# A fused attention and MoE kernel: sread of the first batch moved into the second, its state transposes and token sums re-placed, and its start reordered

## The chip, the cores and the metric

One core of one Trainium2 chip runs the whole program. The metric is device microseconds of that core for one execution, as the median of several. The profile is of one such execution; its span is 1.8 us shorter than the time of its run (222.8 against 224.57 for the kernel before).

All times inside an execution are microseconds from the start of its span. Engine names are the profile's: PE is TensorE, DVE is VectorE, ACT is ScalarE, POOL is GpSimd, SP is the engine that issues the transfers of the outputs and the x transposes by DMA. To evict a result is to copy it from the PSUM bank that a matmul wrote to SBUF; a transfer lands when its completion is recorded.

## The reference, cut to what matters

```python
B, H, S, Ns, D = 8, 8, 512, 32, 64
a     = softmax(scale * x @ state.T)          # over Ns, tokens read the state
xread = a @ state                             # [B, H, S, D]
a2    = softmax(scale * state @ x.T)          # over S, the state reads tokens
sread = a2 @ x                                # [B, H, Ns, D]
h     = rows_of(concat([xread, sread])) @ w_in     # 4352 rows, 512 -> 2048
out   = (h * sigmoid(h)) @ w_out                   # 2048 -> 512
```

For the rows of xread the kernel never forms `xread`: it folds the state into the first weight, W1 = state @ w_in for each batch, and feeds `a` (transposed) to it. So each batch b of 0 to 7 needs scores, exp and a normalisation, W1 in four pieces of 512 columns, 16 steps "ft" of G1 (two matmuls of 512 columns, then SiLU on ACT) and 64 matmuls of G2. The rows of sread are kept as `xmT` and form a ninth, smaller batch at the end.

## The kernel before

The parts that the change and the argument touch. `bank` hands out PSUM banks in turn; `both` is (DVE, ACT); `keep_busy(n, ...)` issues n matmuls on a dummy tile, whose result nobody reads. Parts that are left out are marked with `...`.

```python
def token_sums(b):                       # DVE only, about 2.7 us
    for hg in range(2):
        nc.vector.tensor_reduce(f[:, hg], exp_nat[b, hg] ..., op=ADD)
    nc.vector.tensor_copy(es[b][:, 0], f[:])
    nc.vector.tensor_tensor(es[b][:, 1], f[:], es[b][:, 0], op=SUB)

def sread(b):                            # PE 0.68 us, then DVE about 3.0 us
    ps = bank(...)
    ...  # 2 matmuls of 256 columns with es[b], 16 of 64 columns with x_nat[b] and exp_nat[b]
    nc.vector.reciprocal(rb[:], ps[:, 1, :, :, :])
    ...  # four tensor_tensor products into xmT; the bank is held until they are done

def w1_cols(b, cols, engs):              # one piece: 8 matmuls into two banks, evicted by DVE and ACT
    ...

# start of batch 0
keep_busy(7, psH, "h1"); copy(st0); transpose st0; copies into stT (DVE); keep_busy(4, ...)
cast_x(0, nc.vector, h0=0, nh=4);  pe_transpose_x(0, 0, ...)
cast_x(0, nc.vector, h0=4, nh=4)
scores(0, 0); exps(0, 0)
pe_transpose_x(0, 1, ...);  scores(0, 1); exps(0, 1)
...                                       # SiLU table, normalisation, first 256 columns of W1
pe_transpose_a(0, 0, nc.vector); pe_transpose_a(0, 1, nc.vector)

W0 = {0: (256, 256), 2: (512, 512), 6: (1024, 512), 10: (1536, 512)}
for ft in range(NFT):                     # batch 0
    upto(...)                             # G1 steps that are due
    if ft in W0: w1_cols(0, [W0[ft]], both)
    if ft == 1:  token_sums(0)
    if ft == 4:  sread(0)
    if ft == 5:  transpose_state()        # states of batches 1 to 7
    if ft == 6:  evict_state(0, nc.vector)
    if ft == 8:  evict_state(1, nc.vector)
    if ft == 12: cast_x(1, nc.vector); load_x(2)
    if ft in (9, 11, 12): w1_chunks(1, ({9: 0, 11: 1, 12: 2}[ft],), both)
    if ft == 14: ...                      # transposes of x of batch 1 on PE
    if ft < 14:
        for tt in range(3): G2(0, tt, ft)
```

Transfers: x of batch n+1 is loaded in float32 into the single buffer `x_f` by POOL's queue, cast to bf16 (`x_nat`) and transposed (`xT`), on PE for batches 0 and 1, by DMA from SP's queue from batch 2 on.

The softmax here doesn't subtract the row's maximum and nothing guards it: scores larger than these inputs give would overflow.

Of the kernel before, what the change touches and what calls it, by code (L numbers as in the profile page):

```python
# [8 lines left out]
FP32 = mybir.dt.float32  # L9
BF16 = mybir.dt.bfloat16  # L10
AX = mybir.AxisListType.X
# [25 lines left out]
def kernel(  # L37
# [11 lines left out]
    ctx.enter_context(tc.manual_schedule())  # L49

    pers = ctx.enter_context(tc.tile_pool(name="pers", bufs=1))
    xpool = ctx.enter_context(tc.tile_pool(name="xpool", bufs=2))
    xtpool = ctx.enter_context(tc.tile_pool(name="xtpool", bufs=2))
    att = ctx.enter_context(tc.tile_pool(name="att", bufs=4))
    wpool = ctx.enter_context(tc.tile_pool(name="wpool", bufs=2))
# [41 lines left out]
    def cast_x(b, eng, c0=0, nc_=4, h0=0, nh=H):  # L97
        if b not in x_nat:
            x_nat[b] = xpool.tile([128, 4, H, D], BF16, tag="x_nat", name=f"x_nat{b}")
        eng.tensor_copy(  # L100
            x_nat[b][:, ds(c0, nc_), ds(h0, nh), :],
            x_f[:, ds(h0, nh), ds(c0, nc_), :].rearrange("p h c d -> p c h d"),
        )
# [22 lines left out]
    def keep_busy(n, pool, tag):  # L126
        ps = pool.tile([128, 512], FP32, tag=tag, name="ps_busy")
        for _ in range(n):
            nc.tensor.matmul(  # L129
                ps[:], busy[:, 0:128], busy[:], start=True, stop=True, skip_group_check=True  # L130
            )
# [24 lines left out]
    )  # L156


    keep_busy(7, psH, "h1")
    copy(nc.vector, st0_n[:], st0_f[:])  # L160
    ps0 = bank([128, 4, NS], BF16, "ps_st0")
    for kt in range(4):
# [3 lines left out]
    for g in range(2):  # L166
        for u in range(2):
# [2 lines left out]
                stT[ds(64 * u, 64), 0, ds(2 * g, 2), u ^ g, :],  # L170
                ps0[ds(64 * u, 64), ds(2 * g, 2), :],
            )
    keep_busy(4, psH, "h1")




    def pe_transpose_x(b, hg, nb=2, new=bank, engs=(nc.vector, nc.scalar)):
        if b not in xT:
            xT[b] = xtpool.tile([128, 4, 4, 128], BF16, tag="xT", name=f"xT{b}")  # L180
        m = 4 // nb
        for u in range(nb):
            ps = new([128, m, 2, 128], BF16, "ps_xt")
            for i in range(m):
                for j in range(2):
                    nc.tensor.transpose(
                        ps[:, i, j, :],
                        x_nat[b][:, m * u + i, ds(4 * hg + 2 * j, 2), :],
                        ident[:],
                    )  # L190
            copy(engs[u], xT[b][:, ds(m * u, m), ds(2 * hg, 2), :], ps[:])

    cast_x(0, nc.vector, h0=0, nh=4)
    pe_transpose_x(0, 0, 2, lambda sh, dt, nm: psO.tile(sh, dt, tag="o", name=nm))
    cast_x(0, nc.vector, h0=4, nh=4)

    st_ps = []

# [37 lines left out]
                    skip_group_check=True,  # L236
                )

    def exps(b, hg):
        e = att.tile([128, 4, 4, NS], BF16, tag="exp", name="exp_nat")  # L240
        exp_nat[b, hg] = e
        nc.scalar.activation(e[:], sc_ps[hg][:], func=EXP, bias=0.0, scale=SCALE)  # L242

    an = {}

    def norm(b, hg, parts=((nc.gpsimd, 0, 4),)):
        e = exp_nat[b, hg]
        rs = att.tile([128, 4, 4, 1], FP32, tag="rs", name="rs")
        rc = att.tile([128, 4, 4, 1], FP32, tag="rc", name="rc")
        a = att.tile([128, 4, 4, NS], BF16, tag="an", name="an")  # L250
        an[b, hg] = a
        nc.vector.tensor_reduce(rs[:], e[:], axis=AX, op=ADD)  # L252
        nc.vector.reciprocal(rc[:], rs[:])  # L253
        for eng, c, n in parts:
            eng.tensor_tensor(  # L255
                a[:, ds(c, n)],
                e[:, ds(c, n)],
                rc[:, ds(c, n)].to_broadcast([128, n, 4, NS]),
                op=MULT,
            )  # L260
        if hg == 0:
            aT[b] = att.tile([128, 2, 4, 128], BF16, tag="aT", name="aT")
# [91 lines left out]
    gt = {}  # L354
    outs = {}

    def emit_G1(k):
        b, ft = divmod(k, NFT)
        ps = psH.tile([128, 512], FP32, tag="h1", name="h1")
        if b < B:  # L360
            for hg in range(2):
                nc.tensor.matmul(  # L362
                    ps[:],
                    W1[b][:, hg, ds(128 * ft, 128)],
                    aT[b][:, hg, :, :],
                    start=(hg == 0),
                    stop=(hg == 1),
                    skip_group_check=True,
                )
        else:  # L370
            for kt in range(4):
                nc.tensor.matmul(  # L372
                    ps[:, 0:256],
                    w_in_sb[:, kt, ds(128 * ft, 128)],
                    xmT[:, :, kt].rearrange("p t n b -> p t (n b)"),
                    start=(kt == 0),
                    stop=(kt == 3),
                    skip_group_check=True,
                )
        n = 512 if b < B else 256  # L380
        g = gpool.tile([128, 512], BF16, tag="g", name="g")
        gt[k] = g
        nc.scalar.activation(g[:, 0:n], ps[:, 0:n], func=SILU, bias=0.0)  # L383
# [45 lines left out]
    def upto(k):  # L429
        while done[0] < min(k, (B + 1) * NFT):  # L430
            emit_G1(done[0])
            done[0] += 1

    scores(0, 0)
    exps(0, 0)
    pe_transpose_x(0, 1, 2, lambda sh, dt, nm: psH.tile(sh, dt, tag="h1", name=nm))
    scores(0, 1)
    exps(0, 1)
    nc.scalar.activation(warm[:], warm[:], func=SILU, bias=0.0)
    norm(0, 0)  # L440
    norm(0, 1, ((nc.gpsimd, 0, 2), (nc.vector, 2, 2)))
    w1_cols(0, [(0, 256)], (nc.scalar, nc.scalar))
    load_w_in(1024)
    load_w_out(8, 4)
    load_w_in(1536)
# [1 line left out]
    load_x(1)  # L447
    keep_busy(4, psO, "o")
    pe_transpose_a(0, 0, nc.vector)
    pe_transpose_a(0, 1, nc.vector)  # L450



# [5 lines left out]
    for ft in range(NFT):  # L459
        upto(min(ft + LEAD0[ft], ready))  # L460
        if ft in W0:
            w1_cols(0, [W0[ft]], both)
            ready = sum(W0[ft]) // 128
        if ft == 1:
            token_sums(0)
        if ft == 4:
            sread(0)
        if ft == 5:
            transpose_state()
        if ft == 6:  # L470
            evict_state(0, nc.vector)
        if ft == 8:
            evict_state(1, nc.vector)
        if ft == 12:
            cast_x(1, nc.vector)
            load_x(2)
        if ft in (9, 11, 12):
            w1_chunks(1, ({9: 0, 11: 1, 12: 2}[ft],), both)
        if ft == 14:
            nc.scalar.activation(warm[:], warm[:], func=EXP, bias=0.0)  # L480
            pe_transpose_x(1, 0, 1, engs=(nc.vector,))
            pe_transpose_x(1, 1, 1, engs=(nc.scalar,))
        if ft < 14:
            for tt in range(3):
                G2(0, tt, ft)
# [33 lines left out]
    for b in range(1, B):  # L519
        n = b + 1  # L520
        lead = 4 if b == 1 else 6
        for tt in range(4):
            for ft in range(NFT):
                at = (tt, ft)
                if tt == 0:
                    upto(NFT * b + min(lead + ft, NFT))
                    if b == 1 and ft == 2:
                        token_sums(1)
                if b == 1 and at == (1, 4):
                    sread(1)  # L530
                if n < B:
                    if at == (0, NFT - lead):
                        scores(n, 0)
                        scores(n, 1)
                        exps(n, 0)
                        exps(n, 1)
                        nc.scalar.activation(warm[:], warm[:], func=SILU, bias=0.0)  # L537
                    if at == (1, 0):
                        for hg in range(2):
                            norm(n, hg)  # L540
                            transpose_a(n, hg)
                        if n + 1 < B:
                            for c in range(4):
                                cast_x(n + 1, nc.gpsimd, c, 1)
                        if n + 2 < B:
                            load_x(n + 2)
                    if at == (1, 8):
                        token_sums(n)
                    if at == (3, 8):
                        if n + 1 < B:  # L550
                            transpose_x(n + 1)
                    if at == (3, 10):
                        sread(n)
                    if at == (2, 8):
                        w1_chunks(n, (0, 1), both)
                    if at == (3, 4):
                        w1_chunks(n, (2, 3), both)
                    if tt == 3 and ft % 2 == 1 and ft // 2 < 6:
                        upto(NFT * n + ft // 2 + 1)
                elif tt > 0 and (ft % 3 == 2 or ft == NFT - 1):  # L560
                    upto(min(done[0] + 1, NFT * (B + 1)))
                G2(b, tt, ft)
            store(b, tt, nc.scalar if tt in (1, 2) else nc.vector)
        for ft in range(NFT):
            gt.pop(NFT * b + ft)
# [34 lines left out]
```

## Time and profile before

| what | value | read from |
|---|---|---|
| time, median | 224.54 us (three runs), 224.67 us (six) | runs |
| PE busy | 213.7 us, 96% | page, part 1 |
| first G2 | 14.14 | PE timeline |
| third W1 piece of batch 0 | wanted 22.84, complete run from 23.43 | PE timeline |
| first W1 piece of batch 1 | 27.85 | PE timeline |
| transposes of x of batch 1 | 35.16 | PE timeline |
| scores of batch 2 | 52.51 | PE timeline |
| first G1 of batch 2 | 63.68, after 1.09 us of waiting | PE timeline |

The page of the kernel before, parts 1 and 4 (busy microseconds and share of the span; then what the chain that ended last consists of):

```profile
...
PE 213.7 (96%) x1491; PEld 101.2 (45%) x1491; DVE 104.7 (47%) x183; ACT 142.5 (64%) x241; POOL 46.1 (21%) x64
...
PE 85%; DVE 10%; ACT 1%; issue 1%; POOL 0%; DVEq 0%; POOLq 0%
```

PE is the bound, with DVE a tenth of the chain. Busy time alone does not say that there is nothing to win. The PE timeline of the kernel before (start, length, engine, line and operation, count, and in brackets the idle time before it and what ended it; L numbers are lines of each kernel's own text, so they shift between kernels):

```profile
...
12.16 0.40 PE L272 MATMUL ps_at<-ident,an 128*128 128x128 bf16 x4 [0.84 <-POOL an L255]
...
13.07 0.81 PE L362 MATMUL h<-aT,W 128*128 128x512 bf16 x3 [0.30 <-DVE aT L123]
...
14.14 0.61 PE L391 MATMUL o<-w_out_sb,g 128*128 128x512 bf16 x2
...
17.94 0.60 PE L362 MATMUL h<-aT,W 128*128 128x512 bf16 x2 [0.37 <-DVE W L123]
...
19.46 0.38 PE L293 MATMUL ps_sr<-es,ones 128*128 128x256 bf16 x2
19.68 0.63 PE L303 MATMUL ps_sr<-exp_nat,x_nat 128*128 128x64 bf16 x16
...
22.84 0.39 PE L336 MATMUL ps_w<-w_in_sb,stT 64*32 64x512 bf16 x1
23.43 0.41 PE L336 MATMUL ps_w<-w_in_sb,stT 64*32 64x512 bf16 x7 [0.20 <-DVE xmT L316]
...
27.85 0.41 PE L336 MATMUL ps_w<-w_in_sb,stT 64*32 64x512 bf16 x8 [0.45 <-DVE stT L123]
...
33.09 0.41 PE L336 MATMUL ps_w<-w_in_sb,stT 64*32 64x512 bf16 x8
...
35.16 1.06 PE L186 MATMUL ps_xt<-ident,x_nat 128*128 128x128 bf16 x16
```

Each bracket is PE standing still. It counts from the modelled end of the matmul before, so the loss is larger when read from starts: of the eight matmuls of the third W1 piece the first starts at 22.84 and the second at 23.43, where the eight of the piece at 27.85 all start within 0.34 us, and W1 of batch 1 starts about 0.6 us later than the order before it allows. Who made it wait is in the DVE timeline of the same kernel, in the same format:

```profile
...
14.52 1.97 DVE L282 TENSOR_REDUCE es_f<-exp_nat 128x128 f32<-128x512 bf16 x2
16.52 0.29 DVE L285 CAST es<-es_f 128x256 bf16<-128x256 f32 x1
16.85 0.43 DVE L286 TENSOR_TENSOR es<-es_f,es 128x256 bf16<-128x256 f32 x1
17.20 0.68 DVE L123 CAST W<-ps_w 128x512 bf16<-128x512 f32 x1
20.34 1.76 DVE L312 RECIPROCAL rb<-ps_sr 128x256 f32<-128x256 f32 x1 [2.46 <-PE ps_sr L303]
22.14 1.24 DVE L316 TENSOR_TENSOR xmT<-ps_sr,rb 64x64 bf16<-64x64 f32 x4
...
24.50 3.30 DVE L123 COPY stT<-ps_st 64x224 bf16<-64x224 bf16 x8
```

The copy helper is L123. The first two brackets are the waits for the normalised and transposed a. The eviction of W at 17.20 stands behind the token sums that began at 14.52, and PE's G1 at 17.94 waits for it. The products that end at 23.38 free the bank that PE wants at 22.84. The state copies end at 27.80, and PE starts W1 of batch 1 at 27.85.

### The profile page before, as it was taken

The page shows a single profiled execution, that of the slowest core. Times are in us where ns is not written, and L with a number is a line of the kernel's source. Part 1 is how long each engine was busy: PE and PEld are TensorE (multiplying, and loading weights), DVE is VectorE, ACT ScalarE, POOL GpSimd, SP SyncE. Part 2 cuts the span into 40 slices and gives each one's busy share as a digit, 9 for nine tenths or more (in the row PEclk, how much of TensorE's full clock was granted, in tenths as well). Part 3 has the DMA queues.
Part 4 walks back from the last instruction along what each step waited for, and adds up shares of the span by engine and source line. Part 5 has one row for each costly group of instructions (what it writes and reads, how often), then busy time and mean ns, then how long its engine had stood idle before and what let it go on. Part 6 is the DMA issues. An engine that isn't in the chain of part 4 may idle for free.

```text
span 222.8 us, 3748 instructions
## 1 busy us (share of the span) xinstructions
PE 213.7 (96%) x1491; PEld 101.2 (45%) x1491; DVE 104.7 (47%) x183; ACT 142.5 (64%) x241; POOL 46.1 (21%) x64
## 2 busy tenths in 40 slices
PE   7879899999989999999999999999999999999993
PEld 2425235445425443544444444444454445466652
DVE  4665846452975165525644382629260846010011
ACT  2555469899555985589567947695759675834410
POOL 8480001800810035001800090008000300000000
PEclk9999999999999999999999999999999999999998
DMA  6999955493376116911495138503700330111112
GB/s 184 198 205 206 211 190 174 159 228 113 96 233 139 47 47 121 306 47 47 100 250 125 50 94 242 136 3 105 177 18 35 85 108 0 47 47 50 47 47 94
DMA packets 32209, 26.78 MB, mean 120 GB/s; under 512 B 20160, under 2 KB 26048, under 8 KB 32192
## 3 DMA queue, kind: packets, MB, share of 16 engines
q1 hardware_dynamic: 25376, 14.75, 23.8%
q0 software_dynamic: 6816, 11.80, 23.6%
q8 instruction: 11, 0.18, 0.3%
q14 instruction: 6, 0.05, 0.1%
HBM read 17.37 MB, written 8.91 MB: 118 GB/s over the span
## 4 chain that ended last, share of the span: by engine, by line
PE 85%; DVE 10%; ACT 1%; issue 1%; POOL 0%; DVEq 0%; POOLq 0%
PE o L391 45%; PE h L362 24%; PE ps_w L336 4%; PE h L372 3%; PE ps_busy L129 2%; DVE es_f L282 2%; PE ps_sc L230 2%; PE o_half L413 2%; DVE rb L312 2%; PE ps_sr L303 1%; DVE stT L123 1%; DVE W L123 1%; DVE xmT L316 1%; DVE rs L252 1%; ACT exp_nat L242 1%
## 5 line engine op out<-in xcount | busy, mean ns | idle before, releaser
L391 PE MATMUL o<-w_out_sb,g 128*128 128x512 bf16 x512 | 137.6, 379 | 0.0
L383 ACT ACTIVATE g<-h 128x512 bf16<-128x512 f32 (+1 forms) x144 | 82.1, 574 | 41.4 <-PE h L362 27.2
L362 PE MATMUL h<-aT,W 128*128 128x512 bf16 x256 | 75.5, 379 | 1.9 <-DVE W L123 1.5
L391 PEld LDWEIGHTS <-g 128*128 128x128 bf16 x528 | 49.7, 98 | 58.2 <-issue 6.4
L123 DVE COPY o_sb<-o 128x512 f32<-128x512 f32 x17 | 11.8, 692 | 62.7 <-PE o L391 62.5
L362 PEld LDWEIGHTS <-W 128*128 128x128 bf16 x256 | 24.6, 98 | 32.3 <-DVE W L123 3.7
L255 POOL TENSOR_TENSOR an<-exp_nat,rc 128x512 bf16<-128x512 bf16 (+1 forms) x16 | 16.0, 1010 | 109.8 <-DVE rc L253 109.6
L123 DVE CAST W<-ps_w 128x512 bf16<-128x512 f32 (+1 forms) x31 | 20.0, 675 | 18.7 <-PE ps_w L336 18.7
L121 ACT ACTIVATE W<-ps_w 128x512 bf16<-128x512 f32 (+1 forms) x35 | 18.7, 575 | 11.4 <-PE ps_w L336 11.3
L312 DVE RECIPROCAL rb<-ps_sr 128x256 f32<-128x256 f32 x8 | 14.0, 1749 | 16.2 <-PE ps_sr L303 16.2
L121 ACT ACTIVATE o_sb<-o 128x512 f32<-128x512 f32 x15 | 8.9, 596 | 14.3 <-PE o L391 6.1
L282 DVE TENSOR_REDUCE es_f<-exp_nat 128x128 f32<-128x512 bf16 x16 | 15.5, 1011 | 0.2
L100 POOL CAST x_nat<-x_f 128x512 bf16<-128x512 f32 x24 | 14.7, 648 | 0.0
L336 PE MATMUL ps_w<-w_in_sb,stT 64*32 64x512 bf16 (+1 forms) x264 | 11.7, 376 | 0.6 <-DVE stT L123 0.4
L252 DVE TENSOR_REDUCE rs<-exp_nat 128x16 f32<-128x512 bf16 x16 | 10.6, 660 | 1.9 <-ACT exp_nat L242 1.2
L95 POOL DMA_DIRECT2D x_f<-in_x_dram x7 | 6.5, 926 | 19.8 <-DVE x_nat L100 18.3
L316 DVE TENSOR_TENSOR xmT<-ps_sr,rb 64x64 bf16<-64x64 f32 x32 | 9.6, 299 | 0.6
L372 PE MATMUL h<-xmT,w_in_sb 128*128 128x256 bf16 x64 | 9.6, 272 | 0.0
L242 ACT ACTIVATE exp_nat<-ps_sc 128x512 bf16<-128x512 f32 x16 | 8.8, 594 | 0.9 <-PE ps_sc L230 0.8
L372 PEld LDWEIGHTS <-w_in_sb 128*128 128x128 bf16 x64 | 6.3, 98 | 3.9
L242 ACT ACT_TABLE_LOAD x6 | 7.7, 1283 | 0.1
L537 ACT ACT_TABLE_LOAD x6 | 7.7, 1283 | 0.1
(56 smaller groups left out, 102.7 us busy)
## 6 DMA issues: line engine op xcount, KB each, us to landing
out_dram<-o_sb SPq DMA_DIRECT2D x33, 256.0 KB, 2.4
x_f<-in_x_dram POOLq DMA_DIRECT2D x7, 1024.0 KB, 6.7
w_in_sb<-in_moe_w_in_dram POOLq DMA_DIRECT2D x3, 512.0 KB, 10.2
w_out_sb<-in_moe_w_out_dram POOLq DMA_DIRECT2D x3, 512.0 KB, 12.0
x_f<-in_x_dram SPq DMA_DIRECT2D x2, 512.0 KB, 4.5
w_in_sb<-in_moe_w_in_dram POOLq DMA_DIRECT2D x2, 256.0 KB, 7.3
w_out_sb<-in_moe_w_out_dram POOLq DMA_DIRECT2D x2, 256.0 KB, 7.8
st_b<-in_state_dram POOLq DMA_DIRECT2D x1, 256.0 KB, 12.1
```

The costliest lines, as they stand in the source:

```text
L100: eng.tensor_copy(x_nat[b][:, ds(c0, nc_), ds(h0, nh), :], x_f[:, ds(h0, nh), ds(c0, nc_), :].rearrange("p h c d -> p c h d"),)
L121: nc.scalar.activation(dst, src, func=COPY, bias=0.0)
L123: eng.tensor_copy(dst, src)
L242: nc.scalar.activation(e[:], sc_ps[hg][:], func=EXP, bias=0.0, scale=SCALE)
L255: eng.tensor_tensor(a[:, ds(c, n)], e[:, ds(c, n)], rc[:, ds(c, n)].to_broadcast([128, n, 4, NS]), op=MULT,)
L282: nc.vector.tensor_reduce(f[:, hg], exp_nat[b, hg].rearrange("p c s n -> p s n c"), axis=AX, op=ADD)
L312: nc.vector.reciprocal(rb[:], ps[:, 1, :, :, :])
L336: nc.tensor.matmul(pss[f, hg][ds(32 * s, 32), 0:n], stT[ds(r, 64), b, h // 2, s % 2, :], w_in_sb[ds(r, 64), h // 2, ds(f, n)], start=True, ...
L362: nc.tensor.matmul(ps[:], W1[b][:, hg, ds(128 * ft, 128)], aT[b][:, hg, :, :], start=(hg == 0), stop=(hg == 1), skip_group_check=True,)
L372: nc.tensor.matmul(ps[:, 0:256], w_in_sb[:, kt, ds(128 * ft, 128)], xmT[:, :, kt].rearrange("p t n b -> p t (n b)"), start=(kt == 0), stop ...
L383: nc.scalar.activation(g[:, 0:n], ps[:, 0:n], func=SILU, bias=0.0)
L391: nc.tensor.matmul(outs[tt][:], gt[b * NFT + ft][:, ds(128 * tt, 128)], w_out_sb[:, ft, :], start=(ft == 0), stop=(ft == NFT - 1), skip_gr ...
```

## The change

Its intent: take DVE work that nobody needs yet out of the first 28 us, where PE waits for DVE, and shorten the path from x to the first G1. A third `x_nat` buffer is needed because x of batch 0 must now live until sread in batch 1.

```diff
-    xpool = ... bufs=2
+    xpool = ... bufs=3
-    keep_busy(7, psH, "h1")        # ahead of the first state's transposes
+    keep_busy(4, psH, "h1")
-    keep_busy(4, psH, "h1")        # behind them
+    keep_busy(5, psH, "h1")
-    cast_x(0, nc.vector, h0=0, nh=4)
+    cast_x(0, nc.vector, 0, 2, 0, 4)
+    cast_x(0, nc.scalar, 2, 2, 0, 4)
     pe_transpose_x(0, 0, 2, ...)
-    cast_x(0, nc.vector, h0=4, nh=4)
+    cast_x(0, nc.vector, 0, 2, 4, 4)
+    cast_x(0, nc.vector, 2, 2, 4, 4)
+    pe_transpose_x(0, 1, 2, new_h, (nc.vector, nc.vector), (0,))
     scores(0, 0)
     exps(0, 0)
-    pe_transpose_x(0, 1, 2, ...)
+    pe_transpose_x(0, 1, 2, new_h, (nc.vector, nc.vector), (1,))
     scores(0, 1)
-    exps(0, 1)                     # then SiLU's table, then the normalisation
-    norm(0, 1, ((nc.gpsimd, 0, 2), (nc.vector, 2, 2)))
+    exps(0, 1, 2)                  # in halves; SiLU's table behind the first W1 columns
+    norm(0, 1, ((nc.vector, 0, 3), (nc.gpsimd, 3, 1)), 2)
     ...
     pe_transpose_a(0, 0, nc.vector)
+    keep_busy(2, psO, "o")
     pe_transpose_a(0, 1, nc.vector)
+    g1_half(0, 0)                  # first halves of the first two G1
+    g1_half(1, 0)
     ...
-        if ft == 1:  token_sums(0)
-        if ft == 4:  sread(0)
-        if ft == 5:  transpose_state()
-        if ft == 6:  evict_state(0, nc.vector)
-        if ft == 8:  evict_state(1, nc.vector)
+        if ft == 4:  transpose_state(); evict_state(0, nc.vector)
+        if ft == 6:  evict_state(1, nc.vector)
+        if ft == 10: token_sums(0)
     ...                            # batch 1, at = (tt, ft)
-                if b == 1 and at == (1, 4):
-                    sread(1)
+                if b == 1 and at in ((0, 6), (1, 4)):
+                    sread(at[0])
```

More of the change, by code (lines that the diff above doesn't have):

```diff
@@ L51 @@
     pers = ctx.enter_context(tc.tile_pool(name="pers", bufs=1))
-    xpool = ctx.enter_context(tc.tile_pool(name="xpool", bufs=2))
+    xpool = ctx.enter_context(tc.tile_pool(name="xpool", bufs=3))
     xtpool = ctx.enter_context(tc.tile_pool(name="xtpool", bufs=2))
@@ L99, in cast_x @@
             x_nat[b] = xpool.tile([128, 4, H, D], BF16, tag="x_nat", name=f"x_nat{b}")
-        eng.tensor_copy(
+        copy(
+            eng,
             x_nat[b][:, ds(c0, nc_), ds(h0, nh), :],
@@ L172, with pe_transpose_x @@
             )
-    keep_busy(4, psH, "h1")
-    def pe_transpose_x(b, hg, nb=2, new=bank, engs=(nc.vector, nc.scalar)):
+    keep_busy(5, psH, "h1")
+    def pe_transpose_x(b, hg, nb=2, new=bank, engs=(nc.vector, nc.scalar), only=None):
         if b not in xT:
@@ L181, in pe_transpose_x @@
         m = 4 // nb
-        for u in range(nb):
+        for u in range(nb) if only is None else only:
             ps = new([128, m, 2, 128], BF16, "ps_xt")
@@ L237, in scores, with exps, norm @@
                 )
-    def exps(b, hg):
+    def exps(b, hg, n=4):
         e = att.tile([128, 4, 4, NS], BF16, tag="exp", name="exp_nat")
         exp_nat[b, hg] = e
-        nc.scalar.activation(e[:], sc_ps[hg][:], func=EXP, bias=0.0, scale=SCALE)
+        for c in range(0, 4, n):
+            nc.scalar.activation(
+                e[:, ds(c, n)], sc_ps[hg][:, ds(c, n)], func=EXP, bias=0.0, scale=SCALE
+            )
     an = {}
-    def norm(b, hg, parts=((nc.gpsimd, 0, 4),)):
+    def norm(b, hg, parts=((nc.gpsimd, 0, 4),), nr=4):
         e = exp_nat[b, hg]
@@ L251, in norm @@
         an[b, hg] = a
-        nc.vector.tensor_reduce(rs[:], e[:], axis=AX, op=ADD)
+        for c in range(0, 4, nr):
+            nc.vector.tensor_reduce(rs[:, ds(c, nr)], e[:, ds(c, nr)], axis=AX, op=ADD)
         nc.vector.reciprocal(rc[:], rs[:])
@@ L355, with g1_half @@
     outs = {}
+    h_ps = {}
+    def g1_half(k, hg):
+        b, ft = divmod(k, NFT)
+        if hg == 0:
+            h_ps[k] = psH.tile([128, 512], FP32, tag="h1", name="h1")
+        nc.tensor.matmul(
+            h_ps[k][:],
+            W1[b][:, hg, ds(128 * ft, 128)],
+            aT[b][:, hg, :, :],
+            start=(hg == 0),
+            stop=(hg == 1),
+            skip_group_check=True,
+        )
     def emit_G1(k):
         b, ft = divmod(k, NFT)
-        ps = psH.tile([128, 512], FP32, tag="h1", name="h1")
         if b < B:
-            for hg in range(2):
-                nc.tensor.matmul(
-                    ps[:],
-                    W1[b][:, hg, ds(128 * ft, 128)],
-                    aT[b][:, hg, :, :],
-                    start=(hg == 0),
-                    stop=(hg == 1),
-                    skip_group_check=True,
-                )
+            if k not in h_ps:
+                g1_half(k, 0)
+            g1_half(k, 1)
+            ps = h_ps.pop(k)
         else:
+            ps = psH.tile([128, 512], FP32, tag="h1", name="h1")
             for kt in range(4):
@@ L432, in upto @@
             done[0] += 1
+    new_h = lambda sh, dt, nm: psH.tile(sh, dt, tag="h1", name=nm)
+    pe_transpose_x(0, 1, 2, new_h, (nc.vector, nc.vector), (0,))
     scores(0, 0)
     exps(0, 0)
-    pe_transpose_x(0, 1, 2, lambda sh, dt, nm: psH.tile(sh, dt, tag="h1", name=nm))
+    pe_transpose_x(0, 1, 2, new_h, (nc.vector, nc.vector), (1,))
     scores(0, 1)
-    exps(0, 1)
+    exps(0, 1, 2)
+    norm(0, 0)
+    norm(0, 1, ((nc.vector, 0, 3), (nc.gpsimd, 3, 1)), 2)
+    w1_cols(0, [(0, 256)], (nc.scalar, nc.scalar))
     nc.scalar.activation(warm[:], warm[:], func=SILU, bias=0.0)
-    norm(0, 0)
-    norm(0, 1, ((nc.gpsimd, 0, 2), (nc.vector, 2, 2)))
-    w1_cols(0, [(0, 256)], (nc.scalar, nc.scalar))
     load_w_in(1024)
@@ L463 @@
             ready = sum(W0[ft]) // 128
-        if ft == 1:
-            token_sums(0)
-        if ft == 4:
-            sread(0)
-        if ft == 5:
-            transpose_state()
-        if ft == 6:
-            evict_state(0, nc.vector)
-        if ft == 8:
-            evict_state(1, nc.vector)
+        if ft == 4:
+            transpose_state()
+            evict_state(0, nc.vector)
+        if ft == 6:
+            evict_state(1, nc.vector)
+        if ft == 10:
+            token_sums(0)
         if ft == 12:
```

## The prediction

> **What bounds the kernel now.** TensorE: PE is 96% busy and has 85% of the chain of work that ended last. [...] the PE timeline agrees (two in 0.43 us), so only bubbles can be won. Those in reach lie in batch 0 (PE timeline):
> - the waits for a before the first G1 (0.84 us for POOL, 0.30 us for the aT eviction); the first G2 starts at 14.14;
> - 0.5 us before 17.94: W1 columns 512 to 1023 wait behind the token sums (2.7 us of DVE from 14.52);
> - 0.5 us before 23.43: a PSUM bank held by sread's xmT;
> - 0.6 us before 27.85: w1 of batch 1 waits for the state evictions (DVE 24.50 to 27.80).
>
> A 1.25 us bubble at 62.2 to 63.7 (W behind DVE's work for batch 2) is not touched.
>
> **What the change does, costed from the trace.**
> 1. Start: earlier stT, x cast in halves on DVE and ACT. But x's second half lands only at about 7.16 (issued at 1.7, 5.5 us to landing), and before already casts it at 7.18. Now scores(0,0) follow a transpose of that half: the first exp comes 0.3 us later (8.04 to 8.35), the second 0.4 us earlier; the normalisation's last part is smaller. First full G1 at 12.8 instead of 13.07, first G2 at 13.85: gain 0.3.
> 2. Token sums gone from ft 1: W is evicted right after its matmuls, ACT's part then binds: gain 0.3.
> 3. sread moved: its 0.68 us of PE (19.46 to 20.14) comes back in batch 1: 0. Its bank wait goes: gain 0.5. Its 3.0 us of DVE land near 48, where DVE is idle (47.9 to 54.05): no cost.
> 4. The third W1 piece is then wanted at 21.6, but its weights land at about 21.9 (issue 12.06, 9.9 us to landing). [...] the GB/s row agrees: saturated at about 205 until 28 us. So the landing can't move: loss 0.4.
> 5. State evictions begin 5 us earlier; the wait before w1 of batch 1 goes: gain 0.6.
> 6. Token sums at ft 10 put 2.7 us of DVE between the evictions of W1 piece 4 and of batch 1's second piece. That eviction ends 4.5 us after piece 4's matmuls; batch 1's third piece, which reuses its bank, wants it after 3.7 us: loss 0.9.
>
> Sum: 0.3 + 0.3 + 0.5 - 0.4 + 0.6 - 0.9 = 0.4 us, all on PE's critical path.
>
> **Predicted time:** 224.1 us, 8 in 10 between 223.3 and 224.9. Chances: faster by over 2% 0.01, within 2% 0.98, slower by over 2% 0.01.
>
> **What would show it.** First G2 at 13.6 to 14.1; PE's waits for xmT and stT gone; a wait of 0.2 to 0.6 us at the third W1 piece near 22; a new PE wait of 0.6 to 1.0 us at ps_w on DVE's W near 31 to 32; sread of batch 0 (0.68 us of PE) near 48; the 1.25 us bubble unchanged; PE's work unchanged.
>
> **What would make it wrong.** x's second half gating less than I think (0.4 more gain); the weights landing earlier (0.4 more); token sums fitting into a hole of DVE (0.9 more); DVE so full in batch 1 that the bubble before batch 2 grows (up to 1 us lost).

What the trace has: matmuls of 512 columns start 0.43 us apart for two (18.38 and 18.81), and 201 to 208 GB/s were moved in every stretch from 5 to 26 us. That only bubbles can be won, that DMA was saturated and that the landing can't move are estimates from these numbers.

## The result, and the profile after

The changed kernel took 224.36 us (median of six, 224.20 to 224.62) against 224.67 us (six, 224.41 to 225.01) before. The ratio is 0.9987 with a 95% interval of 0.9974 to 1.0. Ratios here are the mean time of one kernel's fast runs over that of the other's of the same rounds, so not quite the ratio of the medians that I quote. Executions over 1.5% slower than the fastest of the same kernel are left out of the means. Repeated in later rounds (run e5 below), the same kernel was 0.9968 of before. So the gain is small, 0.1% to 0.4%.

The page of the changed kernel, the same two lines:

```profile
...
PE 212.7 (96%) x1491; PEld 100.8 (45%) x1491; DVE 106.0 (48%) x186; ACT 142.7 (64%) x242; POOL 45.7 (21%) x64
...
PE 82%; DVE 7%; DMA 7%; ACT 1%; issue 1%; POOL 1%; SPq 0%; DVEq 0%; ACTq 0%
```

DMA has appeared in the chain that ended last, with 7%. The PE timeline of the changed kernel:

```profile
...
10.78 0.40 PE L279 MATMUL ps_at<-ident,an 128*128 128x128 bf16 x4 [0.67 <-POOL an L262]
...
13.41 0.60 PE L408 MATMUL o<-w_out_sb,g 128*128 128x512 bf16 x2 [0.24 <-ACT g L400]
...
16.89 0.60 PE L370 MATMUL h<-aT,W 128*128 128x512 bf16 x2
...
18.60 0.62 PE L206 MATMUL ps_st<-ident,st_b 128*128 128x128 bf16 x8
...
21.83 0.41 PE L343 MATMUL ps_w<-w_in_sb,stT 64*32 64x512 bf16 x8 [0.45 <-DMA w_in_sb<-in_moe_w_in_dram]
...
25.74 0.41 PE L343 MATMUL ps_w<-w_in_sb,stT 64*32 64x512 bf16 x8
...
30.98 0.39 PE L343 MATMUL ps_w<-w_in_sb,stT 64*32 64x512 bf16 x1
31.76 0.41 PE L343 MATMUL ps_w<-w_in_sb,stT 64*32 64x512 bf16 x7 [0.39 <-DVE W L124]
...
33.84 1.06 PE L187 MATMUL ps_xt<-ident,x_nat 128*128 128x128 bf16 x16
...
47.30 0.38 PE L300 MATMUL ps_sr<-es,ones 128*128 128x256 bf16 x2
47.52 0.63 PE L310 MATMUL ps_sr<-exp_nat,x_nat 128*128 128x64 bf16 x16
```

The wait for the normalised a is shorter, but still there: 0.67 us before 10.78, where it was 0.84. The first G2 waits 0.24 us for SiLU. The third W1 piece waits 0.45 us for the DMA of its own weights. The first W1 piece of batch 1, at 25.74, has no bracket: the state was ready. At 30.98 one matmul of the third piece of batch 1 starts, and the other seven stand until 31.76. The DVE timeline of the changed kernel tells why:

```profile
...
27.74 0.69 DVE L124 CAST W<-ps_w 128x512 bf16<-128x512 f32 x1 [0.83 <-PE ps_w L343]
28.35 1.97 DVE L289 TENSOR_REDUCE es_f<-exp_nat 128x128 f32<-128x512 bf16 x2
30.36 0.29 DVE L292 CAST es<-es_f 128x256 bf16<-128x256 f32 x1
30.69 0.42 DVE L293 TENSOR_TENSOR es<-es_f,es 128x256 bf16<-128x256 f32 x1
31.03 0.68 DVE L124 CAST W<-ps_w 128x512 bf16<-128x512 f32 x1
32.28 1.23 DVE L124 CAST x_nat<-x_f 128x2048 bf16<-128x2048 f32 x1 [0.57 <-DMA x_f<-in_x_dram]
```

The token sums now stand between the two evictions of W, at 27.74 and at 31.03. The bank that the eviction at 31.03 frees is the one PE waits for. In the last line DVE itself waits 0.57 us for x of batch 1 to land.

Following the same marks in both traces shows where the gain came from and where it went. The last column is the difference, that is, how far ahead the changed kernel is at that point:

| mark on PE | before | after | ahead by |
|---|---|---|---|
| first G2 | 14.14 | 13.41 | 0.73 |
| third W1 piece of batch 0 (last seven matmuls before, all after) | 23.43 | 21.83 | 1.60 |
| first W1 piece of batch 1 | 27.85 | 25.74 | 2.11 |
| third W1 piece of batch 1, complete | 33.09 | 31.76 | 1.33 |
| transposes of x of batch 1 | 35.16 | 33.84 | 1.32 |
| scores of batch 2 | 52.51 | 51.87 | 0.64 |
| first G1 of batch 2 | 63.68 | 63.04 | 0.64 |

At its best the changed kernel is 2.11 us ahead. It gives 0.78 us back to the token sums and 0.68 us to sread, which still has to be done, in batch 1. From the scores of batch 2 to the end of the span both kernels take 170.29 us, and e2, e3, e5, e7, e9 and e12 below take 170.25 to 170.29. So in these traces a kernel's span is settled by when the scores of batch 2 start.

### The profile page after: what moved, and what is told of

Its sections match the earlier page's. It is cut to its first block, busy times and chain, and to the rows that moved or that the text cites. A ratio compares the mean times of both kernels' runs of the same rounds, so it can differ in the third digit from the quotient of the medians.

```text
span 222.2 us, 3751 instructions
## 1 busy us (share of the span) xinstructions
PE 212.7 (96%) x1491; PEld 100.8 (45%) x1491; DVE 106.0 (48%) x186; ACT 142.7 (64%) x242; POOL 45.7 (21%) x64
## 4 chain that ended last, share of the span: by engine, by line
PE 82%; DVE 7%; DMA 7%; ACT 1%; issue 1%; POOL 1%; SPq 0%; DVEq 0%; ACTq 0%
PE o L408 45%; PE h L370 23%; DMA w_in_sb<-in_moe_w_in_dram 5%; PE ps_w L343 4%; PE h L389 3%; DMA x_f<-in_x_dram 2%; PE ps_sc L233 2%; DVE es_f L289 2%; PE o_half L430 2%; PE ps_sr L310 1%; DVE W L124 1%; PE ps_xt L187 1%; DVE rb L319 1%; PE ps_sr L300 1%; PE o_a L408 1%
## 5 line engine op out<-in xcount | busy, mean ns | idle before, releaser
L262 POOL TENSOR_TENSOR an<-exp_nat,rc 128x512 bf16<-128x512 bf16 (+2 forms) x16 | 15.8, 1004 | 109.1 <-DVE rc L260 106.0
L259 DVE TENSOR_REDUCE rs<-exp_nat 128x16 f32<-128x512 bf16 (+1 forms) x17 | 10.6, 630 | 1.6 <-ACT exp_nat L246 0.7
L246 ACT ACTIVATE exp_nat<-ps_sc 128x512 bf16<-128x512 f32 (+1 forms) x17 | 8.9, 569 | 1.3 <-PE ps_sc L233 1.2
```

Source lines behind the costliest of these rows:

```text
L246: nc.scalar.activation(e[:, ds(c, n)], sc_ps[hg][:, ds(c, n)], func=EXP, bias=0.0, scale=SCALE)
L259: nc.vector.tensor_reduce(rs[:, ds(c, nr)], e[:, ds(c, nr)], axis=AX, op=ADD)
L262: eng.tensor_tensor(a[:, ds(c, n)], e[:, ds(c, n)], rc[:, ds(c, n)].to_broadcast([128, n, 4, NS]), op=MULT,)
```

## The experiments

Each was timed in five rounds against the kernel before on the same chip. Runs of one call share a chip: e1 to e4, e5 to e8, e9 to e11, and e12. Runs of different calls are compared through their ratios to before. All results were correct, but for e7.

| run | median us | before, same rounds | ratio of fast runs (95%) |
|---|---|---|---|
| the changed kernel, first | 224.36 | 224.67 | 0.9987 (0.9974 to 1.0) |
| e1 start alone | 224.16 | 224.83 | 0.9961 (0.9944 to 0.9977) |
| e2 rest alone | 224.10 | 224.83 | 0.9956 (0.9939 to 0.9972) |
| e3 token sums back in front | 223.89 | 224.83 | 0.9956 (0.9939 to 0.9974) |
| e4 token sums at the tail | 223.83 | 224.83 | 0.9954 (0.9936 to 0.9971) |
| e5 the changed kernel again | 223.91 | 224.77 | 0.9968 (0.9940 to 0.9997) |
| e6 token sums of batch 2 later | 222.87 | 224.77 | 0.9910 (0.9894 to 0.9926) |
| e7 fewer bytes (wrong result) | 224.45 | 224.77 | 0.9981 (0.9963 to 1.0) |
| e8 combination, first try | 227.81 | 224.77 | 1.0134 (1.0114 to 1.0154) |
| e9 sread back | 225.07 | 225.05 | 1.0 (0.9975 to 1.0026) |
| e10 combination, x of batch 3 later | 222.66 | 225.05 | 0.9891 (0.9872 to 0.9910) |
| e11 combination, one x buffer | 225.74 | 225.05 | 0.9931 (0.9888 to 0.9973), three of six runs slow |
| e12 sread's move alone | 224.31 | 224.62 | 0.9979 (0.9965 to 0.9992) |

### e1 and e2: the start alone, the rest alone

The first undoes the second half of the diff above (token sums, sread and state transposes as before); the second undoes the first half (the start as before). With both undone, the order of instructions on every engine is that of the kernel before, and the traces agree: from 13.5 us on at the latest, e1 has the order of before on every engine, and e2 has it up to the first part that was moved. The third x buffer stays in both.

```diff
 # e1, against the changed kernel
-        if ft == 4:  transpose_state(); evict_state(0, nc.vector)
-        if ft == 6:  evict_state(1, nc.vector)
-        if ft == 10: token_sums(0)
+        if ft == 1:  token_sums(0)
+        if ft == 4:  sread(0)
+        if ft == 5:  transpose_state()
+        if ft == 6:  evict_state(0, nc.vector)
+        if ft == 8:  evict_state(1, nc.vector)
-                if b == 1 and at in ((0, 6), (1, 4)): sread(at[0])
+                if b == 1 and at == (1, 4): sread(1)
```
```diff
 # e2, against the changed kernel
-    keep_busy(4, ...) and keep_busy(5, ...); x cast in halves on two engines; exps(0, 1, 2)
-    keep_busy(2, psO, "o");  g1_half(0, 0);  g1_half(1, 0)
+    keep_busy(7, ...) and keep_busy(4, ...); x cast on DVE; scores(0, 0) first; exps(0, 1)
+    norm(0, 1, ((nc.gpsimd, 0, 2), (nc.vector, 2, 2)))
```

> The changes to the start alone (earlier stT, split casts, reordered transposes, halves of exp and sums, g1 halves); token sums, sread and state transposes stay where they were. Theory (weight landings cap what is won): first G2 at about 13.4 us as in the changed kernel, 0.7 earlier than before; without the cap's demand the whole 0.7 reaches the end, since the third W1 piece is wanted only at about 22.1 and its weights land at about 21.8. So about 0.7 us faster than before (224.67), as much as the whole change. Rival (the gains add up): the start is only part of the 0.3 us that the change won, so 0.1 to 0.2 us faster than before.

> The rest alone: token sums at ft 10, sread in batch 1, state transposes at ft 4, third x buffer, with the start of before (first G2 at 14.1). Theory (cap): the third W1 piece starts at about 21.9 as in the changed kernel (21.83), now without a wait for its weights, and everything after it is as in the changed kernel: time within 0.15 us of the changed kernel's 224.36. Rival (the gains add up): the 0.7 us of the start are missing, so about 0.7 us slower than the changed kernel, 225.0.

Measured: each alone is as fast as both together (0.9961 and 0.9956; both together 0.9987 and 0.9968). If the gains added up, both together would be near 0.992. They do not add. In the trace of the rest alone, the third W1 piece starts at 21.92, and in the changed kernel at 21.83, although their first G2 are 0.51 us apart (13.92 and 13.41). Both start 0.05 us after the landing of that piece's weights (21.87 and 21.79, read from the records of the DMA's completion), and so does the piece in e3, e4, e5, e6 and e10: 0.04 to 0.05 us after the landing in all seven traces. The start's lead is spent waiting for weights.

By the medians e1 won 0.67 us, as expected, but its one trace does not show the expected path (first G2 at 13.89, not 13.4). It showed a limit I had not thought of. It is ahead by 0.48 us at the transposes of x of batch 1 (34.68), but its scores of batch 2 start at 52.72, later than before. These are the instructions on the tile xT of batch 2 in e1, with who waited for it and how long its DMA took:

```profile
...
L109 SPq DMA_TRANSPOSE xT<-x_nat x1: 2289/2289/2289, 43.1 to 43.1; - x1
...
  PE ps_sc L233: 0.5, 1
...
DMA to landing us min/median/max: 9.6/9.6/9.6
```

PE waits here for the x transposes by DMA of batch 2, issued at 43.1. This profiled run was the slowest of e1's six (224.69 against 223.75 to 224.29), and the others have no trace, so how often the wait is there is not known, nor what the faster runs of e1 did differently. But it shows that the scores of batch 2 are a second checkpoint that DMA can set. In e2 they too start 0.05 us after the landing (52.12 and 52.08), but there that holds them by only about 0.17 us.

### e3 and e4: where the token sums of batch 0 stand

```diff
-        if ft == 10: token_sums(0)
+        if ft == 1:  token_sums(0)          # e3, as in the kernel before
```
```diff
-        if ft == 10: token_sums(0)
         ...                                 # G2 of the last 128 rows of batch 0, ft == 11
             transpose_x(2)
+            token_sums(0)                   # e4
```

> The changed kernel with the token sums put back at ft 1. Theory: W's eviction before the fifth G1 is late again (0.25 us of PE), but the wait for the third W1 piece's weights takes that up (0.45 to about 0.2 us), and the 0.8 us bank wait before batch 1's third piece goes. How much of it reaches the end is capped by x of batch 1, which lands at about 32.3 and is cast until 33.5: transposes at about 33.6 instead of 33.84, so 0.2 to 0.3 us faster than the changed kernel. Rival (moving the sums back was worth it): 0.2 us or more slower than the changed kernel.

> The changed kernel with the token sums moved further, to the end of batch 0 (after a is transposed, in a hole of DVE). Theory: no bank wait of 0.8 us at batch 1's third piece, which starts at about 31.0 instead of 31.8; then a new wait of about 0.5 us for the cast of x of batch 1 (landing 32.3) before its transposes, at about 33.6. So 0.2 to 0.3 us faster than the changed kernel, not 0.8. Rival (the bank wait alone binds there): transposes at 33.0, 0.8 us faster.

Measured: 223.89 and 223.83 us. Against the changed kernel (0.9968) the ratios 0.9956 and 0.9954 are no difference that the intervals resolve, so in time these two are inconclusive; they exclude neither 0.3 us faster nor none. The rival of e3, 0.2 us or more slower, gets no support. The traces are clear about the mechanism. In e3, the PE timeline reads:

```profile
...
21.70 0.41 PE L343 MATMUL ps_w<-w_in_sb,stT 64*32 64x512 bf16 x8 [0.27 <-DMA w_in_sb<-in_moe_w_in_dram]
...
30.85 0.41 PE L343 MATMUL ps_w<-w_in_sb,stT 64*32 64x512 bf16 x8
...
33.44 1.20 PE L187 MATMUL ps_xt<-ident,x_nat 128*128 128x128 bf16 x16 [0.35 <-DVE x_nat L124]
```

All eight matmuls of batch 1's third piece go out at 30.85; the 0.78 us bank wait is gone. Now x of batch 1 binds: its transposes start 1.31 us after x has landed (32.13), and in e4 also 1.31 us after (32.62, start at 33.93). That is the cast of 1.23 us and its handover. In the changed kernel that distance is 1.59 (32.25, 33.84). So most of the 0.78 us would have been lost to the landing of x anyway.

### e5: the changed kernel again

> The changed kernel once more, unedited, on the same chip as the next three, because its 0.3 us against before came from other rounds than the runs that undo parts of it. If gains do not add up, it lies no more than 0.2 us from the start alone and from the rest alone (0.7 us faster than before each): about 0.7 us faster than before here. If the first measurement holds: 0.3 us faster.

Measured: 223.91 against 224.77, 0.86 us by the medians, ratio 0.9968 with one run at 225.66. That fits the expectation for gains that do not add; the first measurement of 0.3 us was at the low end. The kernel is no faster than its parts, with the reservation that those were timed on another chip.

### e6: the bubble before batch 2

```diff
-                    if at == (1, 8):
+                    if at == ((2, 10) if b == 1 else (1, 8)):
                         token_sums(n)
```

> The changed kernel with the token sums of batch 2 moved behind the first W evictions of batch 2. Theory: the bubble before batch 2's first G1 (about 1.1 us of PE, waiting for DVE's W) comes from DVE's queue, so it goes, and the whole 1.1 us reaches the end: 223.3 where the changed kernel has 224.4. Rival (PE would only wait later, for the second W evictions or for sread of batch 2, since DVE is full there): less than 0.4 us.

Measured: 222.87 against 223.91 for the changed kernel on the same chip, 1.04 us faster. From the scores of batch 2 to its first G1 it is 9.91 us (52.03 to 61.94) instead of 11.17 (51.87 to 63.04). PE's longest waits in the changed kernel and in e6 (in total, times, longest):

```profile
...
PE h L370 <- DVE W L124: 1.1, 1, 1.1
PE ps_xt L187 <- DVE x_nat L124: 1.1, 2, 0.7
...
PE ps_w L343 <- DMA w_in_sb<-in_moe_w_in_dram: 0.5, 1, 0.5
PE ps_w L343 <- DVE W L124: 0.4, 1, 0.4
```

```profile
...
PE ps_xt L187 <- DVE x_nat L124: 1.7, 2, 1.4
...
PE ps_w L343 <- DMA w_in_sb<-in_moe_w_in_dram: 0.4, 1, 0.4
PE ps_w L343 <- DVE W L124: 0.4, 1, 0.4
```

The line of 1.1 us for W is gone from e6, and after the start no new wait took its place. The longer wait for x_nat is at the start and not an effect of the edit: the second half of x landed at 7.12 in e6 and at 6.74 in the other trace. From the scores of batch 2 to the end it is 168.99 us instead of 170.29. This is the largest single gain found, and the change under study did not touch it.

### e7: fewer bytes ahead of the third piece

```diff
-    load_w_out(4, 4)
+    load_w_out(4, 2)
     ...                                     # behind the load of the states
+    nc.gpsimd.memset(w_out_sb[:, 6:8, :], 0.0)
```

> Wrong result on purpose: two of the four w_out blocks of one load are not loaded (zeros instead), which takes about 1.3 us of DMA out of the queue ahead of the state, of the third W1 piece's weights and of x of batch 1. Theory (DMA landings cap batch 0): the waits for the state (0.2) and for the third piece's weights (0.45) go, the third piece starts at about 21.2 and x's landing moves to about 31.0; the bank wait from the token sums (0.8) stays, so the transposes of x of batch 1 start about 0.6 us earlier than 33.84, and the time falls by about 0.6. Rival (PE or DVE bind there, the landings only happen to be close): 0 to 0.2 us.

The 1.3 us of DMA in this expectation are an estimate: the 256 KB left out, at the 205 GB/s of the page. Measured: a miss. The time did not fall: 224.45 against 223.91. In three of the six runs, the profiled one among them, the granted clock was 0.992 instead of 1.0. In the profile, PE's granted clock was 0.88 over the first 14.14 us (0.88 in e4's trace too, 1.00 in the changed kernel's), and the first G2 came at 14.59. The weights land at 19.44, and PE takes the piece at 22.29 without a wait. But that is later than the weights land in the changed kernel with all bytes (21.79), so this trace can't test the theory. Its 7.70 us from the first G2 to the third piece, instead of 8.42, says nothing for the edit either: e8 below, with all bytes and a first G2 at 14.52, has the same 7.70. The other three runs, at full clock (223.99, 224.07, 225.22), were not faster and have no trace. In the trace, x of batch 1 landed at 30.91, but its cast waited on DVE behind the token sums and W's eviction until 32.10, so the next x was loaded no earlier to speak of (33.61, after 33.80). So removing these bytes did not pay by itself; why is not shown. That PE waits for the weights rests on the seven traces under e2, not on this run.

### e8 and e10: a combination, and what a transfer in the wrong place does

e8 takes e4 and e6, casts x of batch 1 in two halves behind W's eviction, and has two float32 x buffers, so that x of batch 2 is loaded right behind x of batch 1. e10 changes one load of e8:

```diff
 # e8
+    xfpool = ... bufs=2                     # x_f, two buffers
     load_x(1)
+    load_x(2)
         if ft == 12:                        # behind w1_chunks
+            cast_x(1, nc.vector, h0=0, nh=4)
+            cast_x(1, nc.vector, h0=4, nh=4)
 # e10, against e8
-            load_x(3)                       # POOL's queue, just ahead of transpose_x(2)
     ...
     store(0, 3, nc.vector)
+    nc.sync.dma_start(x_f of batch 3, x[3])   # SP's queue, behind this store
```

> What the earlier runs point to, together: the changed kernel with the token sums of batch 0 at its end, those of batch 2 behind its W evictions, two buffers for the float32 x (x of batch 2 is loaded right behind that of batch 1) and x of batch 1 cast in two halves, heads 0 to 3 first, after W's eviction. Theory: transposes of x of batch 1 at about 33.0 (0.8 earlier), scores of batch 2 at about 51.0, no bubble of 1.1 us: about 1.9 us faster than the changed kernel. Rival (the x transposes by DMA for batch 2, or the landing of x of batch 1, hold batch 1 where it is): 1.1 to 1.3 us faster.

> The slow combination with one edit: x of batch 3 is loaded behind the last store of batch 0 on SP's queue, at about 45, not from POOL at 41.8. Theory: there the load of x of batch 3 was issued 0.07 us in front of the x transposes by DMA for batch 2 [...], so these took 12.9 us (41.9 to 54.7) instead of about 9 and PE waited 3.7 us. Now they land by 51.5, the wait is under 0.5 us, and the time is 222.0 to 222.4. Rival (two x buffers or the earlier load of x of batch 2 slow it): still above 225.

Measured: e8 is 3 us slower than before, e10 2.4 us faster by the medians. Both theories of e8 were wrong. In e10 the wait for xT is gone, as its theory has it, but the transposes land 5 us earlier than it said, and the median is 0.3 us above its range. The instructions on xT of batch 2 in e8:

```profile
...
L114 SPq DMA_TRANSPOSE xT<-x_nat x1: 3164/3164/3164, 41.9 to 41.9; - x1
...
  PE ps_sc L239: 3.7, 1
...
DMA to landing us min/median/max: 13.4/13.4/13.4
```

And in e10:

```profile
...
L114 SPq DMA_TRANSPOSE xT<-x_nat x1: 1869/1869/1869, 41.9 to 41.9; - x1
...
DMA to landing us min/median/max: 4.4/4.4/4.4
```

The x transposes by DMA are issued at 41.9 in both. In e8 POOL issues the load of x of batch 3 (1 MB) at 41.81, just ahead of them, and they take 13.4 us to land (the 12.9 us in the expectation of e10 are the landing of the load, at 54.73). In the changed kernel that load is issued 0.27 us behind them (42.93 against 42.66), and they take 8.6. In e10 it follows by 3.2 us (45.11), on SP's own queue, and they take 4.4. Freeing a buffer earlier let POOL run earlier (its load at 41.81 instead of 42.93), and that put a 1 MB load 0.07 us ahead of the transposes that PE was about to need. From 45.16 to 64.13 the granted clock was 0.91 in the traces of e8 and e11, where PE waited 3.7 and 2.4 us for xT, and 1.00 in e10's. e10 moved the load in time and to another queue at once; the two are not told apart.

### e9 and e12: what the move of sread is worth

e9 puts sread of batch 0 back into the changed kernel (at ft 4, with the token sums at ft 1, so it compares with e3). e12 moves sread alone, in the kernel before.

```diff
 # e9, against e3
+        if ft == 4: sread(0)                # ahead of transpose_state
-                if b == 1 and at in ((0, 6), (1, 4)): sread(at[0])
+                if b == 1 and at == (1, 4): sread(1)
```
```diff
 # e12, against the kernel before
-    xpool = ... bufs=2
+    xpool = ... bufs=3
-        if ft == 4: sread(0)
-                if b == 1 and at == (1, 4): sread(1)
+                if b == 1 and at in ((0, 6), (1, 4)): sread(at[0])
```

> The changed kernel with sread of batch 0 put back into batch 0 (at ft 4, in front of the state transposes) and so the token sums back at ft 1. To compare with the run that put back the sums alone. Theory: sread's 3 us of DVE (reciprocal and four products) now stand in front of the first state evictions and of the third W1 piece's eviction, so PE waits about 1 us before the ninth G1 (start at about 24.2 instead of 23.0); its 0.68 us of PE is missing in batch 1. The transposes of x of batch 1 start 0.5 to 0.7 us later, scores of batch 2 at about 51.4 to 52.1, where the x transposes by DMA (landing 51.3 to 52.5) may bind: 0 to 0.5 us slower than with the sums alone put back. Rival (sread's move is the heart of the change): over 0.6 us slower.

> The kernel before with one part of the change: sread of batch 0 moved into batch 1, with the third x buffer; start, token sums (ft 1) and state transposes (ft 5) stay. Theory: no bank wait for xmT; the third W1 piece at about 22.2 (weights land at 21.8), w1 of batch 1 still waits about 0.6 us for the state evictions, at about 26.6 instead of 27.85; transposes of x of batch 1 at about 34.0 (35.16 before); scores of batch 2 at about 52.0 instead of 52.5, with sread's 0.68 us in front of them. So 0.5 us faster than before by the chain, and up to 0.9 where the x transposes by DMA for batch 2 land late and sread fills the wait: about as much as the whole change won. Rival (each part carries its own share): 0.2 us or less.

Measured, e12: 0.3 us by the medians and 0.5 by the means (0.9979). Its trace hits the expected marks: third piece 22.21, W1 of batch 1 at 26.64, transposes at 33.96, scores of batch 2 at 52.06. So sread's move alone wins about as much as the change won in its first measurement, and less than in its second.

Measured, e9: no faster than before (1.0), where e3 had 0.9956. That is about 1 us for sread's place, twice the most that I expected; the rival's "over 0.6" fits better. The two runs were on different chips and are compared through before. In e9's trace PE waits longer for W, up to 1.4 us at once, and takes W1 of batch 1 at 27.49 (25.61 in e3):

```profile
...
PE h L370 <- DVE W L124: 2.7, 3, 1.4
...
PE ps_w L343 <- DVE xmT L323: 0.2, 1, 0.2
```

In the profiled runs (224.25 and 223.68, each the fastest of its kernel) the difference is 0.57 us, just above the expected 0 to 0.5. The rest is in slower runs of e9 (up to 225.92) of which there is no trace. Two of the three slowest had a granted clock of 0.991 and 0.992, so part of it may be the clock. Another candidate is the checkpoint that e1 showed: with sread in batch 1, PE has 0.68 us of work to do in front of the scores of batch 2 while the x transposes by DMA are still under way. Both are argued, not shown.

### e11: the combination with one x buffer

```diff
 # against e8
-    two x_f buffers, load_x(2) behind load_x(1)
+    one x_f buffer, load_x(2) behind the cast of x of batch 1 at ft 12
```

> The combination with a single float32 x buffer, as in the changed kernel: token sums of batch 0 at its end, of batch 2 behind its W evictions, x of batch 1 cast in two halves behind W's eviction, x of batch 2 loaded after that. Theory: transposes of x of batch 1 at about 33.2; x transposes by DMA for batch 2 land at 51.3 to 52, against scores wanted at about 51.2, so a wait of 0.1 to 0.8 us: 222.3 to 222.8, up to 0.5 slower than with x of batch 3 moved behind and two buffers. Rival: no difference between the two.

Measured: two kinds of runs. Two took 222.67 and 222.74, like e10; four took 225.09 to 226.76, three of them told as slow. The profile is of a long one, where PE waits 2.4 us for xT of batch 2: x of batch 2 landed at 42.32 instead of 40.29 (after), its cast on POOL and the DMA transposes followed late. The load was issued at 33.80 in both; why it took 8.5 us instead of 6.5 is not shown. What e10 has is that it is steady (222.33 to 223.00 in five runs).

## Why the prediction was right or wrong

The predicted time was 224.1 in a range of 223.3 to 224.9, a gain of 0.4 us. The medians gave 224.36 and 223.91, gains of 0.31 and 0.86, and the two profiles differ by 0.6 us of span. The direction and the size were right, and most steps of the sum were seen at their marks. That the total came out so close is in part luck: steps 1, 2 and 6 are not worth what they say when taken alone, as told below.

1. Start, gain 0.3: right, although the trace shows 0.73. The first G2 comes 6.98 us after the second half of x has landed in the kernel before (7.16 to 14.14) and 6.99 in e2 (6.93 to 13.92), which has the same start; in e12, the third with it, 7.08. It comes 6.67 after it in the changed kernel (6.74 to 13.41), in e1 (7.22 to 13.89) and in e5 (6.49 to 13.16), and likewise in e3, e6, e9 and e11. So the reordering is worth 0.31 us, or 0.4 against e12; the other 0.42 us of the first pair of traces is a landing that happened to come earlier. (In the traces the second half of x landed between 6.49 and 7.24; its cast starts at 6.52 in e5 and at 7.26 in e4.) But e2 against the changed kernel shows that this lead does not get past the third W1 piece when the rest is there (0.51 us ahead before it, 0.09 at it).
2. Token sums gone from ft 1, gain 0.3: G1 at 16.89 is 3.48 us behind the first G2, where it was 3.80 (17.94 less 14.14). Right as part of the sum, but not the token sums' alone: e2, with the sums moved and the old start, has 3.48 too, while e1, e3 and e9, with the new start and the sums left at ft 1, have 3.57 to 3.58. With the old start moving the sums is worth 0.3 us here; with the new start, 0.1.
3. sread's 0.68 us of PE returns in batch 1: seen at 47.30. The bank wait for xmT is gone from PE's waits. Right as a sum of this trace; e9 says that its place is worth more in time than the bank wait.
4. Weights of the third piece, loss 0.4: a wait of 0.45 us for exactly that DMA, at 21.83 (predicted 21.9). The load was issued 0.72 us earlier than before (11.34 and 12.06) and landed only 0.17 us earlier (21.79 and 21.95). The 205 GB/s that the prediction calls saturated is what these loads got, not the most that the engines moved: from 28 to 30 us it was 387 in the kernel before. So that the landing can't move was an estimate, and why it moved so little is not shown. I had missed one of the same kind just ahead: PE takes the state transposes at 18.60, about 0.2 us late, where the states land at 18.55.
5. State evictions, gain 0.6: the wait before W1 of batch 1 is gone. Right.
6. Token sums at ft 10, loss 0.9: 0.78 us between 30.98 and 31.76. Right as a wait. As a loss only about 0.3 us of it counts: x of batch 1 lands only at 32.25, and e3 and e4, without this wait, start its transposes 1.31 us after the landing instead of 1.59.

The bubble before batch 2 was unchanged, as predicted (1.09 us of waiting before, 1.08 after).

What the prediction did not have is a second checkpoint: in e1, e2, e4, e8 and e11 the scores of batch 2, at 52 to 55, are held by the x transposes by DMA. So batch 0 can run between two checkpoints that DMA sets. In neither trace of the changed kernel were the scores held (the landing came 0.62 and 0.29 us ahead of them), so why its gain came out as 0.31 us once and 0.86 the other time stays open. That one transfer delays another is shown only as far as e8 against e10 goes (13.4 and 4.4 us for the same transposes), and e10 changed the queue along with the time.

## What to carry to other kernels

Find the landings first: as long as a later step waits for a transfer whose landing does not move, a faster start in front of it gains nothing at that step, and gains in front of it do not add (here a lead of 0.51 us ahead of the third W1 piece was 0.09 at it). Deferred work has to be set down where its engine has a hole before the next hand-over, so read the queue of the engine that takes it over, not only of the one that is relieved; the largest gain here (1.04 us, e6) was such a queue that the change had left alone. And when a buffer is added or freed earlier, look at which transfer starts earlier because of it, and in front of which one it is issued (here 0.07 us ahead of transposes that then took 13.4 us, against 8.6 where it followed them).

The best version found, e10, takes 222.66 us, 1.1% less than the kernel before, and is correct.
